# The column of sums of phi(k) computed on DVE by a 32x32 block transpose, in place of eight small matmuls on PE

## The chip, the cores and the metric

The kernel runs on one core of a Trainium2 chip. The metric is the device time of one execution in microseconds (us). The profile is one execution seen by the hardware profiler; its span is shorter than the device time of the same execution (163.4 against 165.48 us before). PE is the matmul engine, PEld its weight loads, DVE the vector engine, ACT the scalar engine, POOL is GpSimd. The granted clock is the share of the full PE clock that was let through, 1.00 being all of it.

## The reference, cut to what matters

Two branches are mixed by a gate: a linear attention (A) and a token-mixing MLP (B). The change lies in the denominator of A:

```python
phi = lambda t: jnp.where(t > 0, t + 1, jnp.exp(t)) + 1e-6
pq, pk = phi(q), phi(k)                       # 32 heads of 16, S = 2048, D = 512
kv = jnp.einsum("bhsd,bhse->bhde", pk, v)
z = jnp.einsum("bhsd->bhd", pk)               # <- sum of phi(k) over all 2048 tokens
num = jnp.einsum("bhqd,bhde->bhqe", pq, kv)
den = jnp.einsum("bhqd,bhd->bhq", pq, z)[..., None] + 1e-6
o = num / den
```

## The kernel before

DVE adds the 16 tiles of phi(k) into `zacc` (128 partitions x 512 columns, fp32). What is still missing is the sum over the 128 partitions, and the result is wanted as a column: the 512 sums on the partitions, in four groups of 128. Before, PE did both by multiplying with ones. As PE takes bf16 here, `zacc` was split into a high and a low part.

```python
    def z_split():                      # DVE, when the last tile is added
        nc.vector.tensor_copy(out=zhi[:], in_=zacc[:])
        nc.vector.tensor_tensor(out=zlo[:], in0=zacc[:], in1=zhi[:], op=ALU.subtract)

    def z_matmuls():                    # PE: 8 matmuls of 8 columns, then one DVE write of Z32
        zps = bank("zps")
        for j in range(ND):
            for i, part in enumerate((zhi, zlo)):
                mm(
                    zps[:, 8 * j : 8 * j + 8], part[:, j * P : (j + 1) * P], ones8[:],
                    i == 0, i == 1,
                )
        nc.vector.tensor_tensor(
            out=Z32[:].rearrange("p (j m) -> p j m", m=40)[:, :, 0:8],
            in0=zps[:, 0:32].rearrange("p (j m) -> p j m", m=8),
            in1=maskH[:].unsqueeze(1).to_broadcast([P, ND, 8]), op=ALU.mult,
        )
    ...
    for t in range(11, NT):
        z_add(t)
    z_split()
    ...
    for j in range(NB0, NF):            # blocks of the first MLP matmul, j = 3 .. 13
        c, jj = divmod(j, FB)
        acc = bank("uacc")
        for t in range(NT):
            mm(acc[:], w1c[c][:, t, jj * P : (jj + 1) * P], hs[:, t, :], t == 0, t == NT - 1)
        gelu(j, acc)
        if j == NB0 + 2:
            z_matmuls()
        if j == NB0 + 3:
            kv_matmuls()
            den_matmuls()               # 16 matmuls, the first readers of Z32
            ...
```

## Time and profile before

| | before |
|---|---|
| device time, median of 3 runs | 165.23 us (165.11 to 165.82) |
| profiled span | 163.4 us |
| PE busy | 158.7 us, 97% |
| DVE busy | 88.3 us, 54% |
| granted clock of PE | 1.00 |

These lines are from the page of the kernel before: the span, the busy time of the engines, the clock granted to PE in 40 slices (9 is 90% or more), and the chain of waits that ended last, by engine and by line.

```profile
span 163.4 us, 2099 instructions
...
PE 158.7 (97%) x787; PEld 73.3 (45%) x801; DVE 88.3 (54%) x202; ACT 58.7 (36%) x90; POOL 18.3 (11%) x37
...
PEclk9999999999999999999999999999999999999999
...
PE 95%; DMA 2%; issue 1%; ACT 0%; DVE 0%
PE uacc L108 30%; PE yps L108 29%; PE aps L108 9%; PE gacc L108 8%; PE qacc L108 8%; PE kacc L108 8%; DMA xs<-in_A_x_dram 2%; PE pt L195 1%; PE denps L108 1%; PE wps L108 1%; PE kvps L108 0%; ACT xT L199 0%; DVE ot L481 0%; PE zps L108 0%; 
```

The chain answers what the time is made of: nearly all of it is PE, one matmul group after the other. The list of waits of PE (who waited for whom, us in total, times, longest) has two entries, both at the start of the kernel:

```profile
PE wps L108 <- PEq L502: 0.8, 1, 0.8
PE pt L195 <- DMA xs<-in_A_x_dram: 0.3, 1, 0.3
```

So work on another engine costs nothing until PE has to wait for it. Next is the timeline of PE around the change: start in us, duration in us, then the instruction; a merged line ends with the number of instructions.

```profile
67.19 0.81 PE L108 MATMUL uacc<-hs,w1c 128*128 128x512 bf16 x3
67.83 0.17 PE L108 MATMUL zps<-const-bfloat16-1.0,zhi 128*128 128x8 bf16 x1
67.86 0.17 PE L108 MATMUL zps<-const-bfloat16-1.0,zlo 128*128 128x8 bf16 x1
...
68.01 0.17 PE L108 MATMUL zps<-const-bfloat16-1.0,zlo 128*128 128x8 bf16 x1
68.04 3.61 PE L108 MATMUL uacc<-hs,w1c 128*128 128x512 bf16 x16
71.58 0.69 PE L108 MATMUL kvps<-gT,wv_sb 128*64 128x64 bf16 x32
72.20 0.40 PE L108 MATMUL denps<-pqT,Z 128*32 128x512 bf16 x4
```

The durations mislead here. Each small matmul is listed with 0.17 us, but they overlap: eight start within 0.18 us, and the next uacc matmul follows at 68.04. The three uacc matmuls from 67.19 on show the stream's own distance, (67.83 - 67.19) / 3 = 0.21 us for a listed 0.38. What the eight take from the stream is the distance of the starts, 68.04 - 67.83 = 0.21 us. The first readers of Z are the denps matmuls at 72.20. The timeline of DVE over the same stretch, with the idle time before an instruction and what ended it in brackets:

```profile
59.73 4.32 DVE L270 TENSOR_TENSOR zacc<-zacc,pk 128x512 f32<-128x512 f32 x6
64.08 0.43 DVE L348 CAST zhi<-zacc 128x512 bf16<-128x512 f32 x1
64.54 0.69 DVE L349 TENSOR_TENSOR zlo<-zacc,zhi 128x512 bf16<-128x512 f32 x1
68.22 0.19 DVE L359 TENSOR_TENSOR Z<-zps,maskH 128x32 bf16<-128x32 f32 x1 [2.98 <-PE zps L108]
72.32 0.86 DVE L341 TENSOR_TENSOR kvbdT<-kvps,mask 64x256 bf16<-64x256 f32 x2 [3.91 <-PE kvps L108]
73.31 3.36 DVE L379 RECIPROCAL rden<-denps 128x512 bf16<-128x512 f32 x1
```

After zlo DVE has no work but the short write of Z, and its later steps wait for PE.

### The profile page before, as it was taken

The page shows a single profiled execution, that of the slowest core. Times are in us where ns is not written, and L with a number is a line of the kernel's source. Part 1 is how long each engine was busy: PE and PEld are TensorE (multiplying, and loading weights), DVE is VectorE, ACT ScalarE, POOL GpSimd, SP SyncE. Part 2 cuts the span into 40 slices and gives each one's busy share as a digit, 9 for nine tenths or more (in the row PEclk, how much of TensorE's full clock was granted, in tenths as well). Part 3 has the DMA queues.
Part 4 walks back from the last instruction along what each step waited for, and adds up shares of the span by engine and source line. Part 5 has one row for each costly group of instructions (what it writes and reads, how often), then busy time and mean ns, then how long its engine had stood idle before and what let it go on. Part 6 is the DMA issues. An engine that isn't in the chain of part 4 may idle for free.

```text
span 163.4 us, 2099 instructions
## 1 busy us (share of the span) xinstructions
PE 158.7 (97%) x787; PEld 73.3 (45%) x801; DVE 88.3 (54%) x202; ACT 58.7 (36%) x90; POOL 18.3 (11%) x37
## 2 busy tenths in 40 slices
PE   7999999999999999999999999999999999999993
PEld 2544444444444444444444444444444444444452
DVE  1599999957999999029995301156221111111112
ACT  3463386648676483111222213111112222111110
POOL 5000711200100000001055500050000000000000
PEclk9999999999999999999999999999999999999999
DMA  5999999999950007600893599932100000111001
GB/s 152 235 237 213 280 308 328 349 349 348 326 130 0 0 0 247 202 4 0 286 299 101 181 320 279 323 121 88 36 32 32 32 32 32 45 52 35 32 32 32
DMA packets 30057, 25.05 MB, mean 153 GB/s; under 512 B 7968, under 2 KB 29472, under 8 KB 30048
## 3 DMA queue, kind: packets, MB, share of 16 engines
q1 hardware_dynamic: 28032, 22.02, 45.5%
q0 software_dynamic: 1440, 2.38, 5.5%
q10 hardware_dynamic: 576, 0.52, 1.1%
q8 instruction: 6, 0.10, 0.3%
q14 instruction: 3, 0.02, 0.0%
HBM read 21.11 MB, written 2.23 MB: 143 GB/s over the span
## 4 chain that ended last, share of the span: by engine, by line
PE 95%; DMA 2%; issue 1%; ACT 0%; DVE 0%
PE uacc L108 30%; PE yps L108 29%; PE aps L108 9%; PE gacc L108 8%; PE qacc L108 8%; PE kacc L108 8%; DMA xs<-in_A_x_dram 2%; PE pt L195 1%; PE denps L108 1%; PE wps L108 1%; PE kvps L108 0%; ACT xT L199 0%; DVE ot L481 0%; PE zps L108 0%; PE pt L324 0%
## 5 line engine op out<-in xcount | busy, mean ns | idle before, releaser
L108 PE MATMUL uacc<-hs,w1c 128*128 128x512 bf16 x219 | 51.8, 379 | 0.4
L108 PE MATMUL yps<-uT,w2c 128*128 128x512 bf16 (+2 forms) x234 | 50.6, 366 | 0.2
L481 DVE SCALAR_TENSOR_TENSOR ot<-yps,c,a_sc 128x512 bf16<-128x512 f32 (+2 forms) x17 | 12.2, 720 | 46.0 <-PE yps L108 42.7
L108 PEld LDWEIGHTS <-w2c 128*128 128x128 bf16 x238 | 22.8, 98 | 25.9
L108 PEld LDWEIGHTS <-w1c 128*128 128x128 bf16 x224 | 21.7, 98 | 26.3 <-issue 0.4
L468 ACT ACTIVATE a_sc<-aps,c,gg 128x512 f32<-128x512 f32 x16 | 12.4, 778 | 46.7 <-PE aps L108 43.0
L318 ACT ACTIVATE uT<-uacc,bcol 128x512 bf16<-128x512 f32 x14 | 9.3, 687 | 28.3 <-PE uacc L108 28.3
L108 PE MATMUL aps<-W2sb,pqT 128*128 128x512 bf16 x63 | 16.4, 379 | 0.1
L108 PE MATMUL qacc<-xT,wq_sb 128*128 128x512 bf16 x63 | 16.2, 379 | 0.0
L108 PE MATMUL kacc<-wk_sb,xT 128*128 128x512 bf16 x63 | 16.0, 380 | 0.1
L108 PE MATMUL gacc<-pk,xs 128*128 128x512 bf16 x62 | 15.5, 379 | 0.1
L245 ACT ACTIVATE hs<-xs,nmr,rstd 128x512 bf16<-128x512 bf16 x16 | 12.8, 805 | 1.9 <-DVE nmr L239 1.9
L205 ACT ACTIVATE e<-qacc 128x512 bf16<-128x512 f32 x16 | 9.6, 597 | 9.2 <-PE qacc L108 8.3
L419 POOL DMA_DIRECT2D rex<-rd_dram x16 | 9.4, 602 | 23.0 <-DVE pqT L421 17.5
L205 ACT ACTIVATE e<-kacc 128x512 bf16<-128x512 f32 x16 | 9.3, 595 | 6.9 <-PE kacc L108 5.6
L209 DVE SCALAR_TENSOR_TENSOR pk<-kacc,e 128x512 bf16<-128x512 f32 x16 | 11.1, 692 | 0.6
L209 DVE SCALAR_TENSOR_TENSOR pqT<-qacc,e 128x512 bf16<-128x512 f32 x16 | 11.1, 692 | 0.6
L229 DVE BATCH_NORM_STATS2 stats<-xs 128x6 f32<-128x512 bf16 x16 | 10.9, 682 | 0.0
L206 DVE TENSOR_SCALAR e<-e 128x512 bf16<-128x512 bf16 x32 | 9.0, 282 | 3.1 <-ACT e L205 3.1
L406 DVE CUSTOM_DVE_ANT_0 junk<-xs,gw_b 128x512 bf16<-128x512 bf16 x16 | 9.9, 684 | 0.0
L270 DVE TENSOR_TENSOR zacc<-zacc,pk 128x512 f32<-128x512 f32 x14 | 9.6, 686 | 0.2
L108 PEld LDWEIGHTS <-pqT 128*128 128x128 bf16 x64 | 6.3, 98 | 7.6
(65 smaller groups left out, 69.6 us busy)
## 6 DMA issues: line engine op xcount, KB each, us to landing
w2c<-in_B_w_dram SPq DMA_DIRECT2D x8, 896.0 KB, 6.6
w1c<-in_B_w_dram SPq DMA_DIRECT2D x2, 2048.0 KB, 15.7
w1c<-in_B_w_dram SPq DMA_DIRECT2D x3, 1024.0 KB, 12.9
rex<-rd_dram POOLq DMA_DIRECT2D x16, 128.0 KB, 3.2
out_dram<-ot SPq DMA_DIRECT2D x15, 128.0 KB, 1.7
xs<-in_A_x_dram SPq DMA_DIRECT2D x3, 512.0 KB, 5.1
wq_sb<-in_A_wqkv_dram SPq DMA_DIRECT2D x1, 512.0 KB, 7.1
wv_sb<-in_A_wqkv_dram SPq DMA_DIRECT2D x1, 512.0 KB, 11.4
```

The source lines that it names most:

```text
L108: nc.tensor.matmul(o, lhsT=lhsT, rhs=rhs, start=start, stop=stop, **kw)
L205: nc.scalar.activation(out=e[:], in_=acc[:], func=ACT.Exp)
L206: nc.vector.tensor_scalar(out=e[:], in0=e[:], scalar1=1.0, scalar2=PHI_EPS, op0=ALU.min, op1=ALU.add)
L209: nc.vector.scalar_tensor_tensor(out=dst, in0=acc[:], scalar=0.0, in1=e[:], op0=ALU.max, op1=ALU.add)
L229: nc.vector.bn_stats(out=stats[:], in_=xs[:, t, :])
L245: nc.scalar.activation(out=hs[:, t, :], in_=xs[:, t, :], func=ACT.Identity, scale=rstd[:, t : t + 1], bias=nmr[:, t : t + 1],)
L270: nc.vector.tensor_tensor(out=zacc[:], in0=first, in1=pk[:, t, :], op=ALU.add)
L318: nc.scalar.activation(out=uT[:, j, :], in_=acc[:], func=ACT.Gelu_apprx_tanh, bias=bcol[:, j : j + 1])
L406: nc.vector.tensor_tensor_reduce(out=junk[:], in0=xs[:, t, :], in1=gw_b[:], scale=1.0, scalar=0.0, op0=ALU.mult, op1=ALU.add, accum_out=gp ...
L419: nc.gpsimd.dma_start(out=rex[:], in_=src.unsqueeze(1).to_broadcast([8, HEAD, SC]))
L468: nc.scalar.activation(out=a_sc[:], in_=aps[:], func=ACT.Identity, scale=gg[:, t : t + 1], bias=c2[:, t : t + 1],)
L481: nc.vector.scalar_tensor_tensor(out=ot[:, :W], in0=yps[:, :W], scalar=c1[:, t : t + 1], in1=a_sc[:, cs], op0=ALU.mult, op1=ALU.add,)
```

## The change

The intent is to take the eight matmuls off the busiest engine and to use idle time of DVE. A block transpose turns each 32x32 block of `zacc`; a sum over 32 columns then adds 32 partitions' worth; four copies bring the partial sums of the four partition groups side by side, a second sum adds them, and four more copies spread the result to its place.

```diff
-    zhi = keep([P, D], BF16, "zhi")
-    zlo = keep([P, D], BF16, "zlo")
...
+    zT = keep([P, D], FP32, "zT")          # and zpart, zquad, zsum, zcol; Q32 = 32, NQ = 4, NZ = 16
...
-    def z_split(): ...
-    def z_matmuls(): ...
+    def z_column():
+        nc.vector.transpose(out=zT[:], in_=zacc[:])
+        nc.vector.tensor_reduce(
+            out=zpart[:], in_=zT[:].rearrange("p (b k) -> p b k", k=Q32), op=ALU.add, axis=AX.X
+        )
+        for q in range(NQ):
+            nc.vector.tensor_copy(out=zquad[:, q, :], in_=zpart[q * Q32 : (q + 1) * Q32, :])
+        nc.vector.tensor_reduce(
+            out=zsum[:], in_=zquad[:].rearrange("p q b -> p b q"), op=ALU.add, axis=AX.X
+        )
+        for q in range(NQ):
+            nc.vector.tensor_copy(
+                out=zcol[q * Q32 : (q + 1) * Q32, :],
+                in_=zsum[:].rearrange("p (j q) -> p q j", q=NQ)[:, q, :],
+            )
         nc.vector.tensor_tensor(
             out=Z32[:].rearrange("p (j m) -> p j m", m=40)[:, :, 0:8],
-            in0=zps[:, 0:32].rearrange("p (j m) -> p j m", m=8),
+            in0=zcol[:].unsqueeze(2).to_broadcast([P, ND, 8]),
             in1=maskH[:].unsqueeze(1).to_broadcast([P, ND, 8]), op=ALU.mult,
         )
...
-    z_split()
+    z_column()
...
-        if j == NB0 + 2:
-            z_matmuls()
```

More of the change, by code (lines that the diff above doesn't have):

```diff
@@ L46 @@
     FB = 4
+    Q32 = 32
+    NQ = P // Q32
+    NZ = D // Q32
     assert S == 2048 and D == 512 and F % P == 0
@@ L82 @@
     Z32 = keep([P, ND * 40], BF16, "Z32")
-    zhi = keep([P, D], BF16, "zhi")
-    zlo = keep([P, D], BF16, "zlo")
     zacc = keep([P, D], FP32, "zacc")
-    ones8 = nc.const_aps.tensor(1.0, (P, 8), BF16)
+    zT = keep([P, D], FP32, "zT")
+    zpart = keep([P, NZ], FP32, "zpart")
+    zquad = keep([Q32, NQ, NZ], FP32, "zquad")
+    zsum = keep([Q32, NZ], FP32, "zsum")
+    zcol = keep([P, ND], FP32, "zcol")
     rden = keep([P, SC], BF16, "rden")
@@ L345, in kv_matmuls @@
             )
-    def z_split():
-        nc.vector.tensor_copy(out=zhi[:], in_=zacc[:])
-        nc.vector.tensor_tensor(out=zlo[:], in0=zacc[:], in1=zhi[:], op=ALU.subtract)
-    def z_matmuls():
-        zps = bank("zps")
-        for j in range(ND):
-            for i, part in enumerate((zhi, zlo)):
-                mm(
-                    zps[:, 8 * j : 8 * j + 8], part[:, j * P : (j + 1) * P], ones8[:],
-                    i == 0, i == 1,
-                )
+    def z_column():
[13 more added lines that the diff above has]
+            )
         nc.vector.tensor_tensor(
             out=Z32[:].rearrange("p (j m) -> p j m", m=40)[:, :, 0:8],
-            in0=zps[:, 0:32].rearrange("p (j m) -> p j m", m=8),
+            in0=zcol[:].unsqueeze(2).to_broadcast([P, ND, 8]),
             in1=maskH[:].unsqueeze(1).to_broadcast([P, ND, 8]), op=ALU.mult,
```

## The prediction

> **What bounds the kernel now.** PE: the page has it busy 158.7 of 163.4 us (97%). In the chain of waits that ended last PE has 95% and DVE rounds to 0%. The waits of PE are two stalls at the start, 0.8 and 0.3 us. The granted clock is 1.00. So only PE time counts, unless DVE begins to hold PE up.
>
> **Removed.** On PE: 8 weight loads (95 ns, overlapped) and 8 matmuls of 8 columns. Each is listed with 166 ns, but they are pipelined: the timeline has them starting at 67.83, 67.86 ... 68.01 us and the next uacc matmul at 68.04. That is 0.21 us for all eight. PE does not wait for zhi or zlo there. On DVE: the cast zhi (0.43 us, at 64.08), the subtraction zlo (0.69 us), and the 3.0 us in which DVE waits for PE before it writes Z at 68.22. One PSUM bank allocation goes; later ones move round by one.
>
> **Added, all on DVE, in a row after the last addition to zacc (64.08 us).** Estimates from this trace's durations:
> - block transpose of 512 fp32 columns: 0.69 us, as the fp32 512-column addition (0.686 us). The Trainium skill, "Vector Engine (DVE) Microarchitecture Reference", section 3.8, says the transpose front-end sustains one element per cycle per lane; no run shows it yet.
> - sum of 512 to 16 columns: 0.69 us; "VectorE: DVE Perf Modes", the perf-mode tier table, gives the reduction only the plain rate.
> - eight 32-partition copies of 16 or 4 columns: 0.10 to 0.20 us each (128x16 operations here last 0.17 us and start 0.09 to 0.20 us apart), in all 0.8 to 1.6 us.
> - sum of 64 to 16 columns 0.22 us; the write of Z 0.19 us.
>
> Together 2.6 to 3.4 us in place of 1.3 us. Z should be ready near 67 us; now it is at 68.41 us.
>
> **On the critical path.** None of the DVE part. Between 65.2 and 72.3 us DVE has nothing to do but write Z, whose first reader is the first denps matmul at 72.20 us (about 72.0 after). The chain has 7.9 us of room, more than twice my estimate. What follows (kvbdT at 72.32, reciprocal at 73.31) waits for PE, and shifts 0.2 us earlier. GpSimd is idle between 64 and 74 us, so nothing contends. On PE the 0.21 us leaves the chain and nothing replaces it.
>
> **Predicted time.** 165.23 - 0.21 = 165.0 us, range 164.6 to 165.5: 0.13%, less than the spread of the three runs before (165.11 to 165.82). Chances: faster by over 2% 0.01, within 2% 0.97, slower by over 2% 0.02.
>
> **What would show it right or wrong.** No zps matmul; the usual 0.21 us between the starts of the last uacc matmul of j=5 and the first of j=6. Z written between 66.5 and 68 us. The denps matmuls start near 72.0 us with no wait of PE for DVE. DVE busy rises by 1.3 to 2.1 us, to about 90; PE busy falls by 0.2. Profiled span about 163.2 us. The waits of PE stay the two at the start.
>
> **What would make it wrong.** The fp32 transpose or the strided sums could be several times slower than one element per cycle, or each short copy cost over 0.5 us; a chain beyond 7.9 us would stall PE by the excess. The moved PSUM rotation or shifted SBUF addresses could create a wait that I have not seen. A changed start (first loads, stalls before 7 us) could move the time by a few tenths either way, as much as the gain.

## The result

| | before | after |
|---|---|---|
| device time, median of 6 runs each | 165.57 us (165.11 to 165.82) | 165.33 us (165.09 to 165.48) |
| ratio after to before | | 0.9989, 95% interval 0.9972 to 1.0006 |
| profiled span | 163.4 us | 163.4 us |
| PE busy, DVE busy | 158.7, 88.3 us | 158.9, 90.1 us |

A ratio is the mean time of one kernel's fast runs over that of the other's of the same rounds, so it is not quite the ratio of the medians in the table. Executions over 1.5% slower than the fastest of the same kernel are left out of the means. The interval includes 1. The page of the changed kernel:

```profile
span 163.4 us, 2092 instructions
...
PE 158.9 (97%) x779; PEld 73.2 (45%) x793; DVE 90.1 (55%) x211; ACT 58.7 (36%) x90; POOL 18.3 (11%) x37
...
PEclk9999999999999999999999999999999999999999
...
PE 97%; issue 1%; DVE 0%
```

Its waits of PE:

```profile
PE wps L113 <- PEq L508: 0.8, 1, 0.8
```

PE around the change (the 44 uacc matmuls now run through where zps stood; the 16 denps matmuls wait for nothing):

```profile
61.70 9.88 PE L113 MATMUL uacc<-hs,w1c 128*128 128x512 bf16 x44
71.51 0.69 PE L113 MATMUL kvps<-gT,wv_sb 128*64 128x64 bf16 x32
72.13 1.05 PE L113 MATMUL denps<-pqT,Z 128*32 128x512 bf16 x16
```

And DVE, where the new chain stands between the last zacc and the kvbdT that waits for PE:

```profile
59.85 4.31 DVE L275 TENSOR_TENSOR zacc<-zacc,pk 128x512 f32<-128x512 f32 x6
64.20 0.71 DVE L353 STREAM_TRANSPOSE zT<-zacc 128x512 f32<-128x512 f32 x1
64.94 0.69 DVE L354 TENSOR_REDUCE zpart<-zT 128x16 f32<-128x512 f32 x1
65.66 0.69 DVE L358 COPY zquad<-zpart 32x16 f32<-32x16 f32 x4
66.39 0.25 DVE L359 TENSOR_REDUCE zsum<-zquad 32x16 f32<-32x64 f32 x1
66.68 0.68 DVE L363 COPY zcol<-zsum 32x4 f32<-32x4 f32 x4
67.39 0.19 DVE L367 TENSOR_TENSOR Z<-zcol,maskH 128x32 bf16<-128x32 f32 x1
72.24 0.86 DVE L346 TENSOR_TENSOR kvbdT<-kvps,mask 64x256 bf16<-64x256 f32 x2 [4.66 <-PE kvps L113]
73.23 3.36 DVE L387 RECIPROCAL rden<-denps 128x512 bf16<-128x512 f32 x1
```

Z is written by 67.39 + 0.19 = 67.58 us, 4.5 us before the first denps matmul. The two profiled executions can't be compared by their ends alone, because they start differently: loads land at other times, and the first uacc matmul starts at 33.24 us before and at 33.37 us after. So take the stretch from the first uacc to the first denps matmul. The columns are the stretch and its length, the busy time of each engine with the number of its instructions, the granted clock, the DMA share and GB/s. Before:

```profile
core 0: us, PE busy (x) PEld busy (x) DVE busy (x) ACT busy (x) POOL busy (x), PEclk, DMA share, GB/s
33.24:72.20 38.96, 38.80 (x214) 17.96 (x216) 29.03 (x61) 21.40 (x34) 1.08 (x1) 1.00 0.54 163
```

After:

```profile
33.37:72.13 38.76, 38.60 (x206) 17.74 (x209) 30.84 (x70) 21.41 (x34) 1.08 (x1) 1.00 0.52 157
```

The stretch is 0.20 us shorter, PE is 0.20 us less busy in it, and DVE 1.81 us more. The later start took back 0.13 us of that in this pair of executions. This start varies from one execution to the next by more than the gain: in the profiles the first uacc matmul starts between 32.98 and 33.66 us.

### The profile page after: what moved, and what is told of

The parts are those of the page before. It is cut to its first block, busy times and chain, and to the rows that moved or that the text cites. A ratio compares the mean times of both kernels' runs of the same rounds, so it can differ in the third digit from the quotient of the medians.

```text
span 163.4 us, 2092 instructions
## 1 busy us (share of the span) xinstructions
PE 158.9 (97%) x779; PEld 73.2 (45%) x793; DVE 90.1 (55%) x211; ACT 58.7 (36%) x90; POOL 18.3 (11%) x37
## 4 chain that ended last, share of the span: by engine, by line
PE 97%; issue 1%; DVE 0%
PE uacc L113 30%; PE yps L113 29%; PE kacc L113 9%; PE aps L113 9%; PE gacc L113 8%; PE qacc L113 8%; PE wps L113 2%; PE pt L200 1%; PE denps L113 1%; PE kvps L113 0%; DVE ot L487 0%; PE pt L329 0%
## 5 line engine op out<-in xcount | busy, mean ns | idle before, releaser
L113 PEld LDWEIGHTS <-xT 128*128 128x128 bf16 x64 | 6.4, 100 | 7.6 <-ACT xT L204 0.4
```

What stands on the lines that cost most here:

```text
L113: nc.tensor.matmul(o, lhsT=lhsT, rhs=rhs, start=start, stop=stop, **kw)
```

## The experiments

The theory: only PE's time counts; the eight matmuls cost it the distance of their starts, and the DVE chain is free as long as Z comes before denps is due. Rivals: the matmuls had been free and the small gain is noise; or it came from the PSUM rotation (which of the buffers that `bank(...)` hands out each matmul group gets) or the end of the round trip between PE and DVE; or the new DVE work costs something that hides a larger gain. All kernels gave the reference's result. The distances quoted are those from the first uacc to the first denps matmul, 38.96 us before and 38.76 us after.

### p9: the eight matmuls nine times over

```diff
         for j in range(ND):
-            for i, part in enumerate((zhi, zlo)):
-                mm(...)
+            for _ in range(9):
+                for i, part in enumerate((zhi, zlo)):
+                    mm(...)
```

> The kernel before with its set of eight zps matmuls run nine times over (72 in place of 8, same result). Theory: PE is the limit and each zps matmul takes 26 ns of it, the spacing of their starts, so 64 more cost 64 x 0.026 = 1.7 us (ratio to before about 1.010). Rival 1: they hide in slack of PE and removing them gained nothing: 0 us. Rival 2: each costs the 166 ns that the profile lists: +10.6 us. Rival 3: they cost only their 8 columns at the streaming rate (216 ns for 512 columns, so 3.4 ns each): +0.2 us.

Measured: ratio to before 1.0103 (1.0084 to 1.0123), which is +1.7 us on 165.46. The first and the last of the 72 matmuls:

```profile
68.14 0.17 PE L108 MATMUL zps<-const-bfloat16-1.0,zhi 128*128 128x8 bf16 x1
...
69.92 0.17 PE L108 MATMUL zps<-const-bfloat16-1.0,zlo 128*128 128x8 bf16 x1
```

They start (69.92 - 68.14) / 71 = 25 ns apart, and the distance is 74.11 - 33.55 = 40.56 us, 1.60 us more than before for 64 matmuls: 25 ns each. The rivals "free" (0 us), "166 ns each" (+10.6 us) and "8 columns at the streaming rate" (+0.2 us) fall. The eight matmuls of the kernel before are then worth 8 x 25 ns = 0.20 us, which is the whole of what the change saved on the stretch.

### p9_wide: the same with 128 columns each

```diff
-    zps[:, 8 * j : 8 * j + 8], part[:, j * P : (j + 1) * P], ones8[:],
+    zps[:, P * j : P * j + P], part[:, j * P : (j + 1) * P], warm[:, 0:P],
...                                 # the write of Z reads the first 8 of each 128 columns
```

> As p9, but with 128 columns of ones in each of the 72 matmuls (same result). If the 26 ns of an 8-column matmul are a floor per matmul, a 128-column one should be limited by its columns instead, 216 ns x 128/512 = 54 ns: [...]about 3.8 us over before and 2.1 us over p9. Rival: the weight load (95 ns listed) sets the pace of both: same time as p9.

Measured: ratio 1.0252 (1.0233 to 1.0271), +4.2 us, against 3.8 expected; the distance is 76.17 - 33.25 = 42.92 us, 3.96 us more than before.

```profile
67.84 0.22 PE L108 MATMUL zps<-const-bfloat16-1.0,zhi 128*128 128x128 bf16 x1
...
71.94 0.22 PE L108 MATMUL zps<-const-bfloat16-1.0,zlo 128*128 128x128 bf16 x1
```

The starts are (71.94 - 67.84) / 71 = 58 ns apart. Sixteen times the columns cost 2.3 times as much, so the 25 ns of an 8-column matmul are nearly all a charge per matmul and not the cost of its columns. The weight load does not set the pace of both. Every one of these matmuls has a weight load of its own, so no run tells whether the 25 ns belong to the matmul or to its weight load. The Trainium skill, "TensorE: Matmul & The Clock Gate", section "Wait — 56ns, not 53.3ns?", says that the distance of starts never drops below about 25 ns; this agrees for weights of 128 columns. The 32 kvps matmuls, whose weights are 64 columns wide and which the kernel places side by side in pairs (`tile_position`), start closer, (72.20 - 71.58) / 32 = 19 ns apart on average. From the 25 ns one would expect fewer matmuls to save time in the old way, and narrower ones not; no run tried either.

### d2 and d3: the DVE chain two and three times

```diff
-    z_column()
+    for _ in range(2):      # d3: 3
+        z_column()
```

> The changed kernel with the whole DVE chain (3.4 us) run twice in a row (same result). Theory: the chain is off the critical path with 4.5 us to spare (Z written by 67.58 us, denps starts at 72.13): Z by 71.0 us, no change of time, no wait of PE. Rival: DVE work anywhere delays the kernel through later DVE steps: +3.4 us.

Measured for d2: 165.20 us, ratio to before 0.9982 (0.9965 to 0.9999). The distance is 72.19 - 33.42 = 38.77 us, as after. DVE was busy 93.3 us, 3.2 us more than after, and no wait of PE appeared near denps. A second chain is free; this takes away the rival that the first one cost something.

> The same with the chain run three times: Z by 74.4 us, after the 72.13 us at which denps is due. Theory: PE waits 2.3 us before denps and the time is 2.3 us over the changed kernel's, about 167.6 us; DVE is busy 6.8 us more. Rival 1: DVE is only 55% busy, so it is still free: 0 us. Rival 2: all of it counts: +6.8 us. Also open: whether the granted clock falls after the stall.

Measured for d3: 165.46 us before, and 169.07, 167.12, 166.37 and 167.46 us for d3; ratio of the fast runs 1.0092 (1.0061 to 1.0123). The profiled execution is the 169.07 one, with a granted clock of 0.989. The list of waits of PE now opens with the edge of the slack:

```profile
PE denps L113 <- DVE Z L367: 2.0, 1, 2.0
```

The expected stall was 2.3 us, the measured one 2.0. So the third chain costs what sticks out past the slack, and not its 3.4 us. But in the 169.07 us execution the clock fell too: it was 0.50 from 74.62 to 78.03 us, beginning 0.3 us after the denps matmuls had started at 74.30, and 1.00 before and after. The 166.37 us execution is 0.8 us below the sum of d2's 165.2 and the stall; the start alone moves by 0.7 us between profiled executions, but this one was not profiled, and stays unexplained.

### after_again and pe_back: more rounds, and the PE work put back

pe_back is the changed kernel with eight 8-column matmuls at the old place. Nobody reads them.

```diff
+    def idle_matmuls():
+        zps = bank("zps")
+        for j in range(ND):
+            for i in range(2):
+                mm(zps[:, 8 * j : 8 * j + 8], pk[:, i, j * P : (j + 1) * P], warm[:, 0:8], i == 0, i == 1)
...
+        if j == NB0 + 2:
+            idle_matmuls()
```

> The changed kernel again with more rounds, to see the predicted 0.21 us (0.13%) against the noise, and beside pe_back on the same chip. Theory: ratio to before 0.9987, interval perhaps 0.998 to 1.000. Rival: the matmuls were free, ratio 1.0000 with the profiles showing the same distance from the first uacc matmul to the first denps matmul (before 38.96 us, theory 38.75 us).

Measured: ratio 1.0001 (0.9989 to 1.0012). The 0.13% is inside the interval, and so is zero: device times of this many rounds do not resolve it. The trace does: 72.16 - 33.40 = 38.76 us again, in an execution of its own.

> The changed kernel, with eight matmuls of the old size put back at the old place into a PSUM bank that nobody reads (weights from pk, so they wait for nothing; same result). It has the DVE chain of after, the PE work and the PSUM rotation of before. Theory: only the PE work counts, so the ratio to before is 1.000 and the distance from the first uacc to the first denps matmul is 38.96 us again. Rival: the gain came from the end of the round trip from PE to DVE or from the PSUM rotation or SBUF addresses: ratio 0.9987, or something else, as in after.

Measured: ratio 0.9999 (0.9981 to 1.0018), inconclusive for the same reason; its runs spread from 164.82 to 165.80 us. These lines are its first uacc and its denps matmuls:

```profile
33.66 0.81 PE L113 MATMUL uacc<-hs,w1c 128*128 128x512 bf16 x3
...
72.63 1.05 PE L113 MATMUL denps<-pqT,Z 128*32 128x512 bf16 x16
```

The distance is 72.63 - 33.66 = 38.97 us: the PE work alone brings back the 0.2 us, with the DVE chain in place. pe_back also has the old PSUM rotation, so by itself it does not part the two; but p9 has the rotation of before, and charges 25 ns for each matmul, which leaves nothing for the rotation to explain.

### early_pe and early_dve: both ways where Z is wanted at once

The readers of Z are moved from the end of block j=6 (72.2 us) to the end of j=4 (64.6 us), just when zacc is done. First in the kernel before, then in the changed one:

```diff
-        if j == NB0 + 2:
-            z_matmuls()            # early_dve has no such lines
+        if j == NB0 + 1:
+            z_matmuls()            # early_dve: den_matmuls() alone
+            den_matmuls()
         if j == NB0 + 3:
             kv_matmuls()
-            den_matmuls()
```

> The kernel before with the zps and denps matmuls moved from the blocks j=5 and j=6 to the end of j=4 (about 64.6 us), where Z is wanted at once (same result). Here latency counts: zlo is done at 65.2 us, then the matmuls and the write of Z, so denps starts near 65.7 us; PE stalls about 1.0 us: 166.4 us.

Measured: 166.76 us, ratio to before 1.0086 (1.0072 to 1.0101): +1.4 us, where 1.0 was expected. PE at this place:

```profile
64.46 0.18 PE L108 MATMUL zps<-const-bfloat16-1.0,zhi 128*128 128x8 bf16 x1
65.19 0.18 PE L108 MATMUL zps<-const-bfloat16-1.0,zlo 128*128 128x8 bf16 x1 [0.55 <-DVE zlo L349]
...
65.80 1.05 PE L108 MATMUL denps<-pqT,Z 128*32 128x512 bf16 x16 [0.28 <-DVE Z L359]
67.01 3.19 PE L108 MATMUL uacc<-hs,w1c 128*128 128x512 bf16 x14 [0.16 <-issue]
```

From the first zps matmul to the next uacc are 67.01 - 64.46 = 2.55 us, against 0.21 + 0.98 us for the same matmuls in the kernel before: 1.36 us lost. The estimate had denps at 65.7, 0.1 us early; from the last zps matmul (65.35) through the write of Z on DVE to denps (65.80) go 0.45 us. It left out what comes after: from denps to the next uacc are 67.01 - 65.80 = 1.21 us, 0.23 us more than in the kernel before.

> The changed kernel with denps moved to the same place. Its chain needs 3.4 us from the last zacc against about 1.5 us of the old way, so Z comes at 67.6 us and PE stalls 3.0 us: 168.3 us, near 1.9 us slower than early_pe. The same change then is a loss where its latency is exposed. Rival: if the ways are equal once Z is wanted at once, the two runs differ by 0.2 us only.

Measured: 169.75, 168.66, 169.83 and 168.06 us, ratio 1.0226 (1.0190 to 1.0262). The two executions with a clock of 1.00 have 168.06 and 168.66 us, about the 168.3 expected; the other two have 0.99. The denps matmuls of the profiled execution (clock 0.99):

```profile
67.52 1.90 PE L113 MATMUL denps<-pqT,Z 128*32 128x512 bf16 x16 [2.96 <-DVE Z L367]
```

Latency decides here. The chain on DVE starts at 64.08 and denps at 67.52: 3.4 us. In early_pe the cast starts at 63.98 and denps at 65.80: 1.8 us. So the same change, at a place without slack, loses 1.3 to 1.9 us against early_pe even at the full clock, and more when the clock falls. (early_pe has no execution with a clock under 0.999.)

### d3_again, d3_warm, early_dve_again, early_dve_warm: does the stall lower the clock?

A low clock after a stall was not forecast; the expectation of d3 had named it as open. The warm variants fill PE's wait with matmuls of constants that nobody reads:

```diff
+            fill = bank("fill")
+            for _ in range(10):          # early_dve_warm: 14
+                mm(fill[:], warm[:, 0:P], warm[:], True, True)
             den_matmuls()
```

> d3 unchanged, for more executions beside d3_warm on one chip. In d3's profiled execution the 2.0 us stall was followed by about 3.5 us at a lower granted clock, and the time was 169.07 us, where the other three executions took 166.4 to 167.5. Theory: the stall alone costs 2.0 us (near 167.3 us), and in some executions a lowered clock adds up to 1.8 us: times spread from about 167 to 169 us.

> d3 with ten 512-column matmuls of constants into a bank nobody reads between the kvps and the denps matmuls (10 x 0.216 = 2.16 us), so that PE works instead of idling while it waits for Z (same result). Theory: clock 1.00 in every execution and a narrow spread at 165.3 + 2.2 = 167.5 us, none above 168. Rival: the slow executions of d3 are the chip's own slow state and come here as well, or the clock falls for another reason than the idle time.

Measured on one chip: d3_again 167.08 to 167.53 us in five executions at clocks of 0.998 or 0.999, and 169.26 us in one at 0.988; that one is in its ratio, 1.0124 (1.0088 to 1.0160). d3_warm 167.33 to 167.80 us, four of four at 0.999 or more, ratio 1.0126 (1.0107 to 1.0145). The profiled execution of d3_again had the same 2.0 us stall as d3 and kept its clock. Two low executions of ten in d3 and none of four in d3_warm decide nothing, so the question went to the longer stall:

> early_dve unchanged, beside early_dve_warm on one chip. Two of its four executions had a granted clock of 0.99 and took 169.8 us, the others had 1.00 and took 168.1 and 168.7. Theory: the 3.0 us idle stretch of PE lets the clock fall for some 3.5 us in about half of the executions: two groups of times, near 168.3 and 169.8 us, in order of their clocks.

> early_dve with fourteen 512-column matmuls of constants into a bank nobody reads ahead of denps (14 x 0.216 = 3.0 us), so that PE is not idle while it waits for Z (same result). Theory: one group of times only, near 165.35 + 3.1 = 168.4 us, clock 1.00 in every execution. Rival: the low clock has another cause, and about half of the executions show 0.99 and 169.8 us again.

Measured on one chip: early_dve_again 169.65 to 171.37 us, all six at clocks of 0.979 to 0.990, ratio 1.0291 (1.0261 to 1.0320); half of them had been expected. early_dve_warm 168.04 to 168.72 us, five of five at 0.997 or more, ratio 1.0178 (1.0155 to 1.0202). Stretches of the profiled executions, first early_dve_again (PE idle to 67.8 us; the clock is the number behind the busy times):

```profile
64.00:67.00 3.00, 0.86 (x4) 0.20 (x2) 2.79 (x9) 0.69 (x1) 0.00 (x0) 1.00 1.08 362
67.00:70.00 3.00, 2.18 (x17) 0.60 (x18) 0.92 (x6) 0.00 (x0) 0.00 (x0) 0.60 0.39 123
70.00:73.00 3.00, 3.00 (x13) 1.33 (x12) 3.00 (x1) 0.00 (x0) 0.00 (x0) 0.83 0.00 0
73.00:163.00 90.00, 90.00 (x449) 41.10 (x448) 28.44 (x69) 20.56 (x30) 10.09 (x17) 1.00 0.32 107
```

And early_dve_warm:

```profile
64.00:67.00 3.00, 3.00 (x15) 1.38 (x14) 2.77 (x10) 0.69 (x1) 0.00 (x0) 1.00 1.08 363
67.00:70.00 3.00, 3.00 (x26) 1.14 (x25) 1.75 (x5) 0.00 (x0) 0.00 (x0) 1.00 0.28 90
70.00:73.00 3.00, 3.00 (x16) 1.36 (x14) 2.26 (x1) 0.56 (x1) 0.45 (x1) 1.00 0.02 5
```

The idle kernel loses its clock; the kernel that does useless work through the same wait does not. The numbers 0.60 and 0.83 are averages over 3 us: looked at more closely, the clock is 0.50 from 67.60 to 71.01 us, so it falls 2.7 us after PE went idle and while it still waits. In early_dve it is 0.50 from 67.29 to 70.70 us. In all three profiles with a low clock behind a stall it is half the full one for 3.41 us, which takes 1.7 us of PE work away. With early_dve that is eight low executions of ten against none of five. So at this place it is the idle time of PE that brings the low clock, and not a state of the chip of its own. The penalty beyond the stall is the difference of the two means, 170.2 - 168.4 = 1.8 us (1.6 without the 171.37 us execution), in line with the 1.7 us. The mean clock of the 171.37 us execution, 0.979 over 169.5 us, would by the same sum be 3.6 us lost, about two such stretches: an estimate, as it was not profiled. Why six of six fell on one chip and two of four on another, and why a 2.0 us stall only sometimes does it, stays open.

No experiment points to a version that beats both kernels: PE has no wait left at this place, and the 0.20 us were all that the zps matmuls held.

## Why the prediction was right

- "PE ... only PE time counts": d2 adds 3.2 us of DVE work for nothing, p9 pays for every small matmul. Right.
- "That is 0.21 us for all eight", read from starts and not from durations: 0.20 us on the trace of the changed kernel, 25 ns each in p9, 0.21 us back in pe_back. Right. The gain of the time itself (0.9989, then 1.0001) is within its interval both times and is not shown by the times alone. The level, 165.0 us predicted and 165.33 measured, proves little: the median of the kernel before went from 165.23 to 165.57 us with three more runs, more than the gain, and that the time fell into the range of 0.9 us was no test of the mechanism.
- The terms of the DVE chain: transpose 0.71 us (0.69 said), first sum 0.69 (0.69), eight copies 1.4 (0.8 to 1.6), second sum 0.25 (0.22), write of Z 0.19 (0.19); Z at 67.58 us (66.5 to 68), DVE busy up by 1.8 us (1.3 to 2.1). Right. The claims taken from the Trainium skill fit: 512 fp32 columns go through the transpose in 0.71 us and through the sum in 0.69 us, like the plain addition's 0.69 us; one size alone does not part the rate from a fixed time.
- "None of the DVE part" on the critical path, "7.9 us of room": the first extra chain was free, the second stuck out by 2.0 us. Right, in size too.
- "PE busy falls by 0.2": it does in the stretch (38.80 to 38.60 us), but the page of the whole kernel has 158.9 against 158.7. In the first 7.1 us the kacc matmuls are listed with 490 ns in place of 388 ns, and the weight loads among them show a gap of 0.27 us: busy time of PE can hold a wait. The prediction trusted this number too far.
- "Profiled span about 163.2": 163.4, as the first uacc matmul came 0.13 us later. The prediction had named a changed start as a thing of the gain's own size. "The waits of PE stay the two at the start": only one of them was still listed.

## What to carry to other kernels

Cost a small matmul by the distance between starts in the stream, not by its listed duration, and count how many there are; at 8 columns the width hardly matters (25 ns each), at 128 it does (58 ns). Work moved from the limiting engine to an idle one is worth just what it took from the limiting one, and is free only while its latency fits between the last input and the first reader: here 3.4 us in a gap of 7.9 us, and a loss of over a microsecond where the gap was taken away. A stall of PE can cost more than its length, because the clock may fall with it (here to half for 3.4 us, 1.7 us of work); and when a gain is smaller than the spread of the start, compare a stretch between two fixed instructions, not the whole time.

## What the Trainium skill lacked or had wrong

- "TensorE: Matmul & The Clock Gate", section "Why this matters for your kernels", advises against gaps of PE over about 3 us. Here a gap of 3.0 us came with a low clock in 8 of 10 executions (0.50 for 3.41 us in the two of them that were profiled); filled with matmuls, the clock stayed at 0.997 or more in five of five. A gap of 2.0 us came with one in 2 of 10, which is too few to show that the gap was the cause. If it was, the gap is to be kept shorter than the page says.
- The same page, section "Back-to-back issue gap", gives for streams of weight load and matmul a sustained 81 ns at 128 columns and 131 ns at 512. Here 128-column matmuls, each with its own weight load, start 58 ns apart; the 512-column stream is at (67.83 - 67.19) / 3 = 0.213 us, close to what the page gives for the isolated gap (216 ns).
- "VectorE: DVE Perf Modes", section "The three transpose paths", times a bf16 128x128 transpose only. A 128x512 fp32 one took 0.71 us here.
- No page has a time for short copies between groups of 32 partitions: 32x16 and 32x4 copies took 0.16 us each and started (0.69 - 0.16) / 3 = 0.18 us apart, while two independent 128x16 operations that start on the same group (the gate's, near 99.3 us of the kernel before) started 0.09 us apart. The section "Two Vector instructions with no wait between them" of that page says that a change of the starting group holds an instruction until the earlier ones are done. That fits; no run here tells it from another cause.
- No page shows a sum over the partitions that stays on VectorE. Here a 32x32 block transpose, two sums along the columns and eight copies between groups of 32 partitions do it for 128x512 fp32, with the write of Z, in 67.58 - 64.20 = 3.4 us.
